# The opening of a fused attention and MLP kernel, reordered slice by slice

## The chip, the cores and the metric

The kernel runs on one core of a Trainium2 chip. A core has five engines, each with its own instruction stream: TensorE (PE, matrix products; its weight loads are listed apart as PEld), VectorE (DVE), ScalarE (ACT), GpSimd (POOL) and SyncE (SP, which here only starts transfers). They meet through semaphores. The time is that of one execution on the device, in microseconds (us); lower is better. Three executions of the kernel before took 1382.28, 1385.5 and 1387.74 us, so the median is 1385.5 us.

## The reference

One normalized input feeds a 32-head attention block and an MLP; both results are added to the input. S is 2048 tokens, D is 640, a head has 20 columns, the MLP's inner width is 1536.

```python
def _A_ref(x, wqkv, wo):                      # attention
    qkv = (x @ wqkv).reshape(B, S, 3, H, Dh).transpose(2, 0, 3, 1, 4)
    q, k, v = qkv[0], qkv[1], qkv[2]
    scores = jnp.einsum("bhqd,bhkd->bhqk", q, k) * (Dh ** -0.5)
    p = _softmax(scores, axis=-1)
    o = jnp.einsum("bhqk,bhkd->bhqd", p, v)
    return o.transpose(0, 2, 1, 3).reshape(B, S, D) @ wo

def _B_ref(x, w1, b1, w2, b2):                # MLP on a second layer norm
    y = _layernorm(x, axis=-1)
    h = _gelu(jnp.einsum("bsd,df->bsf", y, w1) + b1)
    return jnp.einsum("bsf,fd->bsd", h, w2) + b2

xn = _layernorm(x, axis=-1)
return x + _A_ref(xn, A_wqkv, A_wo) + _B_ref(xn, B_w1, B_b1, B_w2, B_b2)
```

## The kernel before

The inputs are 32-bit floats. For the projections each 32-bit factor is split into two 16-bit parts, a high part (written by ACT as a rounded copy) and a low part (written by DVE as the difference), and a product is the sum of three passes: high by high, high by low, low by high (`PASS`, line 275). A weight is first multiplied by a power of two that follows from its sum of squares.

The program has two parts. The first (lines 155 to 509) projects to Q, K and V; the second (from line 512) is attention, with the MLP and the output projection woven in. Both are written under a manual schedule: every engine runs its instructions in the order in which the text issues them, and what holds an instruction back is only a semaphore of another engine or of a transfer. A tile is taken from a pool with a fixed number of buffers, so a new tile may have to wait for the readers of an old one.

In the first part the 2048 tokens go in four chunks `c` of 512, a chunk as four row tiles `j` of 128 tokens. The steps of a chunk:

- `norm_a` (line 220): mean and variance of each row tile on DVE, a power on POOL. `norm_b` (236): one Newton step, then the four row tiles are normalized in place on DVE (line 243), then three small operations that prepare the second layer norm, the last of them a power on POOL (247). `norm_c` (249): a Newton step for the second norm and a small write by SP.
- `transp` (256) transposes normalized rows on PE into a PSUM tile, two column blocks `k` of 128 at a time; `transp_out` (266) writes high and low parts into `xnts[c]`.
- `qk(c, tt)` (277): one tile of the projection, 256 of the 1280 columns of Q and K, as 2 blocks `i` by 5 blocks `k` by 3 passes, 30 matmuls. Tiles 0 and 1 are columns of Q alone, tile 2 takes the last 128 columns of Q and the first 128 of K. `qk_out` (293): high part on ACT, low part on DVE, squares, and two writes by SP to a scratch in DRAM. `lengths` (313) sums the squares of the tiles that are pending, on PE.
- `vproj` and `vproj_out` (343, 355): the same for V, one row tile at a time.

Before a weight can be split (`split_qkv`, 379), its sum of squares is taken on ACT (`sums`, 368) and turned into a scale (`scale_of`, 371): a matmul with ones on PE (line 110) and seven small operations on DVE (from line 111).

`warm(n)` (205) gives PE n products of ones whose result isn't used; each is two matmul instructions in the profile. The opening (lines 444 to 459) is: filler, statistics of chunk 0, sum for Q, normalization, transposes, scale for Q, filler, the three feature outputs, and then Q's whole split, in five slices of 640 columns. In the main loop, chunk 0, `tt = 0` holds K's sum, `norm_c(0)` and K's scale; `tt = 1` holds K's split, `norm_a(1)` and the load of the MLP's second weight into the buffer in which K's weight stood; `tt = 2` holds V's sum, `norm_b(1)` and V's scale; from `tt = 2` on the transposes of the next chunk follow each tile. PSUM pool `psS` has three buffers of two banks, `psM` and `psO` one bank each.

`brow` (line 202) is a row constant which POOL fills (446) and which SP writes out at line 458.

Of the kernel before, what the change touches and what calls it, by code (L numbers as in the profile page):

```python
# [7 lines left out]
F32 = mybir.dt.float32  # L8
F16 = mybir.dt.float16
BF16 = mybir.dt.bfloat16  # L10
# [6 lines left out]
P = 128  # L17
# [25 lines left out]
def mha_mlp_kernel(tc, x, wqkv, wo, w1, b1, w2, b2, out):  # L43
# [4 lines left out]
    with (  # L48
# [106 lines left out]
        with tc.tile_pool(name="pa", bufs=2) as pa, tc.tile_pool(name="pa1", bufs=1) as pa1, tc.manual_schedule():  # L155
# [39 lines left out]
            for m in range(KD):  # L195
# [4 lines left out]
                                        compare_op=ALU.is_ge, fill=0.0, base=DH - 1 - m * P,  # L200
                                        channel_multiplier=-1)
            brow = pa1.tile([H, S], F16, name="brow")
            lmx = pa1.tile([P, 2, 4], F32, name="lmx")

            def warm(n):
# [30 lines left out]
            def norm_b(c):  # L236
                mv, ve, r, r2 = rs[c]
                newton(r, ve, "a")

                nc.vector.tensor_mul(ve, r, r)  # L240
                nc.vector.tensor_scalar(r, r, 1024.0, None, ALU.mult)
                for j in range(4):
                    nc.vector.tensor_scalar(xts[c][j], xts[c][j], mv[:, j, 0:1], r[:, j : j + 1],
                                            ALU.subtract, ALU.mult)
                nc.vector.tensor_mul(ve, ve, mv[:, :, 1])
                nc.vector.tensor_scalar(ve, ve, EPS, None, ALU.add)
                nc.gpsimd.tensor_tensor(r2, ve, nhalf, ALU.pow)
# [26 lines left out]

            PASS = ((0, 0), (0, 1), (1, 0))

            def qk(c, tt):
                ps = psS.tile([P, 2, 512], F32, tag="s", name="qkp")
                order = [(i, k) for i in range(2) for k in range(KD)]
                if c + tt == 0:  # L280

                    order = [(i, k) for k in range(KD) for i in range(2)]
                for i, k in order:
                    q, mm = divmod(2 * tt + i, KD)
                    for n, (a, b) in enumerate(PASS):
                        nc.tensor.matmul(ps[:, i, :], wv[:, k, q, a, mm * P : (mm + 1) * P],  # L286
                                         xnts[c][:, k, b, :], start=(k + n == 0), stop=(k == KD - 1 and n == 2))
                return ps

            norms = [None, None]  # L290
# [2 lines left out]
            def qk_out(c, tt, ps):  # L293
                hl = stp.tile([P, 2, 2, 512], F16, tag="ks", name="qkhl")

                parts = ((0, 2),) if tt != 2 else ((0, 1), (1, 2))
                sq = pa.tile([P, 2, 512], BF16, tag="sq", name="sq", bufs=2)
                for i0, i1 in parts:
                    a = qks[:, (2 * tt + i0) // KD : (2 * tt + i0) // KD + 1]
                    nc.scalar.activation(hl[:, 0, i0:i1], ps[:, i0:i1], AF.Copy, scale=a)  # L300
                    nc.vector.scalar_tensor_tensor(hl[:, 1, i0:i1], ps[:, i0:i1], a, hl[:, 0, i0:i1],  # L301
                                                   ALU.mult, ALU.subtract)
                if c == 0:
                    nc.scalar.activation(sq, hl[:, 0], AF.Square)
                else:
                    nc.vector.tensor_mul(sq, hl[:, 0], hl[:, 0])
                for s in range(2):
                    nc.sync.dma_start(
                        qkscr[s, 2 * tt * P : (2 * tt + 2) * P, c * 512 : (c + 1) * 512]
                        .rearrange("(i p) t -> p i t", p=P), hl[:, s])  # L310
                pend.extend((c, 2 * tt + i, sq[:, i]) for i in range(2))

            def lengths():
# [54 lines left out]
            def sums(tag, ws):  # L368
                accs[tag] = squares(ws, junk)
# [6 lines left out]
                    q = "qk".index(tag)  # L376
                    nc.vector.tensor_scalar(qks[:, q : q + 1], pw[tag][0], QKTOP, 2.0**-22, ALU.min, ALU.mult)

            def split_qkv(n):
                q = "qkv".index(n)  # L380
                for k in range(KD):
                    nc.scalar.activation(wv[:, k, q, 0], stage[n][:, k], AF.Copy, scale=scales[n])
                    nc.vector.scalar_tensor_tensor(wv[:, k, q, 1], stage[n][:, k], scales[n], wv[:, k, q, 0],
                                                   ALU.mult, ALU.subtract)

            gscale, f1, f2, ch, fo, big = (sc[:, i : i + 1] for i in range(6))

# [55 lines left out]

            warm(40)
            norm_a(0)
            nc.gpsimd.memset(brow, KROW)
            sums("q", [stage["q"][:, 0:3], stage["q"][:, 3:]])
            norm_b(0)
            pts = []
            transp(0, 0, pts)  # L450
            scale_of("q")
            transp(0, 2, pts)
            transp(0, 4, pts)
            warm(12)
            for t in pts:
                transp_out(*t)
            split_qkv("q")
            nc.sync.dma_start(bscr[H : H + 1, :], brow[0:1, :])
            nc.sync.dma_start(b1t, b1.rearrange("(k p) -> p k", p=P))
            for c in range(4):  # L460
                nxt = c + 1 if c < 3 else None
                for tt in range(5):
                    ps = qk(c, tt)
                    lengths()

                    if c == 0:
                        if tt == 0:
                            sums("k", [stage["k"][:, 0:3], stage["k"][:, 3:]])
                            norm_c(0)
                            scale_of("k")  # L470
                        elif tt == 1:
                            split_qkv("k")
                            norm_a(1)
                            nc.sync.dma_start(w2t, w2.rearrange("(k p) n -> p k n", p=P))
                        elif tt == 2:
# [607 lines left out]
```

## Time and profile before

| what | value |
|---|---|
| median of three executions | 1385.5 us |
| the profiled execution, its own time | 1385.2 us |
| its span (first to last instruction) | 1383.5 us |
| mean granted TensorE clock over the span | 0.997 |
| ACT busy | 1126.2 us (81%) |
| DVE busy | 1061.7 us (77%) |
| moved by DMA | 125.68 MB |
| first matmul of the projections | 21.16 us |
| first scores of attention | 232.47 us |

The engines' busy times overlap, so they don't add up to the span. Times in the timeline are microseconds from the span's start. A group's row gives its busy time, the mean time of one instruction in nanoseconds, and behind the second bar the idle time of its engine just before it with what ended most of that. In a timeline row the part in brackets is the idle time before the row and its releaser. Matmul ends are modelled.

### The profile page before, as it was taken

The page shows a single profiled execution, that of the slowest core. Times are in us where ns is not written, and L with a number is a line of the kernel's source. Part 1 is how long each engine was busy: PE and PEld are TensorE (multiplying, and loading weights), DVE is VectorE, ACT ScalarE, POOL GpSimd, SP SyncE. Part 2 cuts the span into 40 slices and gives each one's busy share as a digit, 9 for nine tenths or more (in the row PEclk, how much of TensorE's full clock was granted, in tenths as well). Part 3 has the DMA queues.
Part 4 walks back from the last instruction along what each step waited for, and adds up shares of the span by engine and source line. Part 5 has one row for each costly group of instructions (what it writes and reads, how often), then busy time and mean ns, then how long its engine had stood idle before and what let it go on. Part 6 is the DMA issues. An engine that isn't in the chain of part 4 may idle for free.

```text
span 1383.5 us, 29113 instructions
## 1 busy us (share of the span) xinstructions
PE 1350.8 (98%) x11711; PEld 600.9 (43%) x11711; DVE 1061.7 (77%) x1425; ACT 1126.2 (81%) x1282; POOL 32.9 (2%) x75
## 2 busy tenths in 40 slices
PE   9999999999999999999999999999999999999998
PEld 6555555443333343433343333343334334333375
DVE  6648743899778977889887789877988897888642
ACT  5644323999999999999999999999999999999700
POOL 2000000000000000000000000000000000000000
PEclk9999999999999999999999999999999999999999
DMA  9853413012124231213221123212124322341375
GB/s 265 243 175 109 108 52 110 16 32 64 41 55 111 67 88 34 69 52 102 71 77 33 47 75 103 76 47 58 44 64 113 98 56 70 85 153 59 98 235 179
DMA packets 92320, 125.68 MB, mean 91 GB/s; under 512 B 16905, under 2 KB 58569, under 8 KB 92178
## 3 DMA queue, kind: packets, MB, share of 16 engines
q1 hardware_dynamic: 89218, 117.14, 28.3%
q0 software_dynamic: 2304, 5.24, 2.3%
q8 instruction: 94, 1.54, 0.5%
q10 hardware_dynamic: 656, 1.36, 0.3%
q14 instruction: 48, 0.39, 0.1%
HBM read 80.84 MB, written 42.86 MB: 89 GB/s over the span
## 4 chain that ended last, share of the span: by engine, by line
PE 59%; DVE 11%; ACT 5%; DMA 3%; issue 2%; SPq 1%; DVEq 0%; ACTq 0%
PE o L615 23%; PE s L584 14%; PE py L819 9%; PE pu L787 8%; DVE low L598 5%; PE z L896 5%; ACT p L586 4%; DMA oscr<-oa 1%; DVE u L740 1%; DMA oa<-opart 1%; DVE u L741 1%; DVE w L744 1%; DVE w L745 1%; DVE hT L752 1%; DVE u L750 1%
## 5 line engine op out<-in xcount | busy, mean ns | idle before, releaser
L586 ACT ACTIVATE p<-s 128x1024 f32<-128x1024 f32 x1024 | 973.6, 1042 | 52.4 <-PE s L584 46.2
L598 DVE TENSOR_TENSOR low<-p 128x1024 f16<-128x1024 f32 x512 | 608.8, 1219 | 165.0 <-ACT p L586 164.9
L615 PE MATMUL o<-p,vfull 128*32 128x512 bf16 (+1 forms) x4096 | 433.7, 494 | 0.0
L584 PE MATMUL s<-qs,ks 61*128 61x512 f16 x2048 | 317.7, 382 | 8.7 <-ACT p L586 7.2
L584 PEld LDWEIGHTS <-ks 61*128 61x128 f16 x2048 | 63.9, 94 | 296.4 <-issue 294.2
L787 PE MATMUL pu<-xm,w1t 128*128 128x256 f16 x1440 | 179.2, 274 | 4.1 <-DVE u L740 3.6
L819 PE MATMUL py<-w2t,hT 128*128 128x320 f16 x1152 | 178.6, 301 | 1.7 <-DVE xb L757 1.7
L787 PEld LDWEIGHTS <-w1t 128*128 128x128 f16 x1440 | 130.9, 98 | 71.2 <-issue 57.6
L819 PEld LDWEIGHTS <-hT 128*128 128x128 f16 x1152 | 102.5, 98 | 89.5 <-issue 55.2
L286 PE MATMUL qkp<-xnt,wv 128*128 128x512 f16 x600 | 132.3, 380 | 0.0
L615 PEld LDWEIGHTS <-vfull 128*32 128x32 f16 x3072 | 61.5, 95 | 146.2 <-issue 115.4
L615 PE MATMUL o<-low,vfull 128*32 128x512 f16 x1024 | 107.3, 379 | 6.6 <-DVE low L598 6.4
L300 ACT ACTIVATE qkhl<-qkp,qks 128x1024 f16<-128x1024 f32 (+1 forms) x24 | 23.3, 971 | 84.1 <-PE qkp L286 66.2
L286 PEld LDWEIGHTS <-wv 128*128 128x128 f16 x600 | 58.2, 98 | 67.8
L615 PEld LDWEIGHTS o<-p,vfull 128*32 128x32 f32 x2048 | 63.1, 109 | 50.6 <-issue 0.5
L349 PE MATMUL vp<-wv,xnt 128*128 128x320 f16 x480 | 66.6, 300 | 0.0
L896 PE MATMUL z<-w1t,ot 128*128 128x320 f16 x480 | 65.8, 300 | 0.0
L896 PEld LDWEIGHTS <-ot 128*128 128x128 f16 x480 | 46.7, 98 | 19.8 <-issue 1.7
L349 PEld LDWEIGHTS <-xnt 128*128 128x128 f16 x480 | 46.5, 98 | 18.2
L301 DVE SCALAR_TENSOR_TENSOR qkhl<-qkp,qks,qkhl 128x1024 f16<-128x1024 f32 (+1 forms) x24 | 26.5, 1104 | 34.3 <-ACT qkhl L300 34.3
L857 DVE SCALAR_TENSOR_TENSOR acc<-z,sc,acc 128x320 f32<-128x320 f32 x32 | 17.6, 550 | 45.1 <-PE z L896 42.9
L636 ACT ACTIVATE ev<-o 128x512 f32<-128x512 f32 x64 | 39.4, 615 | 3.3 <-PE o L615 3.3
(168 smaller groups left out, 685.7 us busy)
## 6 DMA issues: line engine op xcount, KB each, us to landing
qkscr<-qkhl SPq DMA_DIRECT2D x40, 256.0 KB
opart<-ev SPq DMA_DIRECT2D x124, 80.0 KB
ks<-qkscr SPq DMA_DIRECT2D x120, 80.0 KB
qs<-qkscr SPq DMA_DIRECT2D x192, 40.0 KB
oa<-opart SPq DMA_DIRECT2D x32, 240.0 KB
xt<-in_A_x_dram SPq DMA_DIRECT2D x16, 320.0 KB
xscr<-xnt SPq DMA_DIRECT2D x4, 1280.0 KB
xm<-xscr SPq DMA_DIRECT2D x8, 640.0 KB
```

Source lines behind the costliest of these rows:

```text
L286: nc.tensor.matmul(ps[:, i, :], wv[:, k, q, a, mm * P : (mm + 1) * P], xnts[c][:, k, b, :], start=(k + n == 0), stop=(k == KD - 1 and n == 2))
L300: nc.scalar.activation(hl[:, 0, i0:i1], ps[:, i0:i1], AF.Copy, scale=a)
L301: nc.vector.scalar_tensor_tensor(hl[:, 1, i0:i1], ps[:, i0:i1], a, hl[:, 0, i0:i1], ALU.mult, ALU.subtract)
L349: nc.tensor.matmul(ps[:, hf, :320], xnts[c][:, k, a, j * P : (j + 1) * P], wv[:, k, 2, b, hf * 320 : (hf + 1) * 320], start=(n == 0), stop ...
L584: nc.tensor.matmul(ps[:, a, :], ks[64 * a : 64 * a + 61, kb * P : (kb + 1) * P], qs[64 * a : 64 * a + 61, cc * 512 : (cc + 1) * 512], star ...
L586: nc.scalar.activation(pt, ps, AF.Exp, scale=QS)
L598: nc.vector.tensor_sub(low, pt, upper(pt))
L615: nc.tensor.matmul(pv.o[32 * q : 32 * q + 32, :], src[:, v0 - PAD * (1 - q % 2) :][:, :32], t, start=q not in pv.begun, stop=last, skip_gr ...
L636: nc.scalar.activation(evs[g, hf][:, cc], pv.o, AF.Copy)
L787: nc.tensor.matmul(ps[:, i], w1v[:, k, (f + i) // 4, a, fo_ : fo_ + P], xnt[:, k, b, :], start=(n == 0), stop=(n == 3 * KD - 1))
L819: nc.tensor.matmul(ps[:, :320], hTs[mc][:, f, a, j * P : (j + 1) * P], w2v[:, f, b, hf * 320 : (hf + 1) * 320], start=(n == 0), stop=(n == ...
L896: nc.tensor.matmul(ps[:, :320], ot[:, k, a, j * P : (j + 1) * P], wov[:, k, b, h * 320 : (h + 1) * 320], start=(n == 0), stop=(n == 3 * KD ...
```

## The change

Some work of the opening is cut into slices and given another place:

- The fill of `brow` on POOL goes from behind `norm_a(0)` to the tile's declaration, behind the masks `heads`.
- The last three operations of `norm_b` become `norm_b2`. For chunks 1 to 3 they stay where they were; for chunk 0 they go, with `norm_c(0)`, to the start of `tt = 1`.
- Chunk 0's transposes go row tile by row tile: four blocks of a row tile together, the scale for Q ahead of the last row tile, and the fifth block of all four row tiles at the end, in a tile of `psM`. The filler behind them is 10 products instead of 12.
- Features and Q's weights come in turn: for each `k`, block `k` of the features (512 columns, high and low) and then slice `k` of Q's weights, only the 256 columns of the first tile. Columns 256 to 511 are split behind the first tile's matmuls, columns 512 to 639 in `tt = 1`.
- `tt = 0` ends after K's sum of squares. The rest of it moves into `tt = 1`, in this order: `norm_b2(0)`, `norm_c(0)`, the second tile's matmuls with K's scale issued from among them (`mid`, behind block `i = 1` of `k = 2`, so behind 18 of 30 matmuls), the first tile's `qk_out` without the squares, the last columns of Q, K's split, `lengths` (nothing is pending), the first tile's squares (`qk_sq`), `norm_a(1)`, the load of the MLP's second weight, the second tile's `qk_out`.
- The second tile's matmuls go, as the first's did, with `k` in the outer loop.

```diff
@@ -200,6 +200,7 @@
                                         compare_op=ALU.is_ge, fill=0.0, base=DH - 1 - m * P,
                                         channel_multiplier=-1)
             brow = pa1.tile([H, S], F16, name="brow")
+            nc.gpsimd.memset(brow, KROW)
             lmx = pa1.tile([P, 2, 4], F32, name="lmx")
 
             def warm(n):
@@ -242,6 +243,11 @@
                 for j in range(4):
                     nc.vector.tensor_scalar(xts[c][j], xts[c][j], mv[:, j, 0:1], r[:, j : j + 1],
                                             ALU.subtract, ALU.mult)
+                if c > 0:
+                    norm_b2(c)
+
+            def norm_b2(c):
+                mv, ve, r, r2 = rs[c]
                 nc.vector.tensor_mul(ve, ve, mv[:, :, 1])
                 nc.vector.tensor_scalar(ve, ve, EPS, None, ALU.add)
                 nc.gpsimd.tensor_tensor(r2, ve, nhalf, ALU.pow)
@@ -274,10 +280,10 @@
 
             PASS = ((0, 0), (0, 1), (1, 0))
 
-            def qk(c, tt):
+            def qk(c, tt, mid=None):
                 ps = psS.tile([P, 2, 512], F32, tag="s", name="qkp")
                 order = [(i, k) for i in range(2) for k in range(KD)]
-                if c + tt == 0:
+                if c == 0 and tt < 2:
 
                     order = [(i, k) for k in range(KD) for i in range(2)]
                 for i, k in order:
@@ -285,6 +291,8 @@
                     for n, (a, b) in enumerate(PASS):
                         nc.tensor.matmul(ps[:, i, :], wv[:, k, q, a, mm * P : (mm + 1) * P],
                                          xnts[c][:, k, b, :], start=(k + n == 0), stop=(k == KD - 1 and n == 2))
+                    if mid and (i, k) == (1, 2):
+                        mid()
                 return ps
 
             norms = [None, None]
@@ -294,20 +302,25 @@
                 hl = stp.tile([P, 2, 2, 512], F16, tag="ks", name="qkhl")
 
                 parts = ((0, 2),) if tt != 2 else ((0, 1), (1, 2))
-                sq = pa.tile([P, 2, 512], BF16, tag="sq", name="sq", bufs=2)
                 for i0, i1 in parts:
                     a = qks[:, (2 * tt + i0) // KD : (2 * tt + i0) // KD + 1]
                     nc.scalar.activation(hl[:, 0, i0:i1], ps[:, i0:i1], AF.Copy, scale=a)
                     nc.vector.scalar_tensor_tensor(hl[:, 1, i0:i1], ps[:, i0:i1], a, hl[:, 0, i0:i1],
                                                    ALU.mult, ALU.subtract)
+                if c + tt > 0:
+                    qk_sq(c, tt, hl)
+                for s in range(2):
+                    nc.sync.dma_start(
+                        qkscr[s, 2 * tt * P : (2 * tt + 2) * P, c * 512 : (c + 1) * 512]
+                        .rearrange("(i p) t -> p i t", p=P), hl[:, s])
+                return hl
+
+            def qk_sq(c, tt, hl):
+                sq = pa.tile([P, 2, 512], BF16, tag="sq", name="sq", bufs=2)
                 if c == 0:
                     nc.scalar.activation(sq, hl[:, 0], AF.Square)
                 else:
                     nc.vector.tensor_mul(sq, hl[:, 0], hl[:, 0])
-                for s in range(2):
-                    nc.sync.dma_start(
-                        qkscr[s, 2 * tt * P : (2 * tt + 2) * P, c * 512 : (c + 1) * 512]
-                        .rearrange("(i p) t -> p i t", p=P), hl[:, s])
                 pend.extend((c, 2 * tt + i, sq[:, i]) for i in range(2))
 
             def lengths():
@@ -376,12 +389,12 @@
                     q = "qk".index(tag)
                     nc.vector.tensor_scalar(qks[:, q : q + 1], pw[tag][0], QKTOP, 2.0**-22, ALU.min, ALU.mult)
 
-            def split_qkv(n):
+            def split_qkv(n, ks=range(KD), c0=0, c1=D):
                 q = "qkv".index(n)
-                for k in range(KD):
-                    nc.scalar.activation(wv[:, k, q, 0], stage[n][:, k], AF.Copy, scale=scales[n])
-                    nc.vector.scalar_tensor_tensor(wv[:, k, q, 1], stage[n][:, k], scales[n], wv[:, k, q, 0],
-                                                   ALU.mult, ALU.subtract)
+                for k in ks:
+                    nc.scalar.activation(wv[:, k, q, 0, c0:c1], stage[n][:, k, c0:c1], AF.Copy, scale=scales[n])
+                    nc.vector.scalar_tensor_tensor(wv[:, k, q, 1, c0:c1], stage[n][:, k, c0:c1], scales[n],
+                                                   wv[:, k, q, 0, c0:c1], ALU.mult, ALU.subtract)
 
             gscale, f1, f2, ch, fo, big = (sc[:, i : i + 1] for i in range(6))
 
@@ -443,33 +456,51 @@
 
             warm(40)
             norm_a(0)
-            nc.gpsimd.memset(brow, KROW)
             sums("q", [stage["q"][:, 0:3], stage["q"][:, 3:]])
             norm_b(0)
-            pts = []
-            transp(0, 0, pts)
-            scale_of("q")
-            transp(0, 2, pts)
-            transp(0, 4, pts)
-            warm(12)
-            for t in pts:
-                transp_out(*t)
-            split_qkv("q")
+            xnts[0] = pa.tile([P, KD, 2, 512], F16, tag="xnt", name="xnt0")
+            pts = [psS.tile([P, 2, 512], F32, tag="s", name="pt") for _ in range(2)]
+            pt = [pts[0][:, 0], pts[0][:, 1], pts[1][:, 0], pts[1][:, 1]]
+            for j in range(4):
+                if j == 3:
+                    scale_of("q")
+                    pt.append(psM.tile([P, 512], F32, tag="m", name="pt4"))
+                for k in range(KD - 1):
+                    nc.tensor.transpose(pt[k][:, j * P : (j + 1) * P], xts[0][j][:, k * P : (k + 1) * P], ident)
+            for j in range(4):
+                nc.tensor.transpose(pt[4][:, j * P : (j + 1) * P], xts[0][j][:, 4 * P :], ident)
+            warm(10)
+
+            for k in range(KD):
+                nc.scalar.activation(xnts[0][:, k, 0, :], pt[k], AF.Copy)
+                nc.vector.tensor_sub(xnts[0][:, k, 1, :], pt[k], xnts[0][:, k, 0, :])
+                split_qkv("q", [k], 0, 2 * P)
+            nc.sync.dma_start(xscr[:, :, :, :512], xnts[0])
+            del xts[0]
             nc.sync.dma_start(bscr[H : H + 1, :], brow[0:1, :])
             nc.sync.dma_start(b1t, b1.rearrange("(k p) -> p k", p=P))
             for c in range(4):
                 nxt = c + 1 if c < 3 else None
                 for tt in range(5):
-                    ps = qk(c, tt)
+                    if c == 0 and tt == 1:
+                        norm_b2(0)
+                        norm_c(0)
+                        ps = qk(0, 1, lambda: scale_of("k"))
+                        hl = qk_out(0, 0, first)
+                        split_qkv("q", c0=4 * P)
+                        split_qkv("k")
+                    else:
+                        ps = qk(c, tt)
                     lengths()
 
                     if c == 0:
                         if tt == 0:
+                            split_qkv("q", c0=2 * P, c1=4 * P)
                             sums("k", [stage["k"][:, 0:3], stage["k"][:, 3:]])
-                            norm_c(0)
-                            scale_of("k")
+                            first = ps
+                            continue
                         elif tt == 1:
-                            split_qkv("k")
+                            qk_sq(0, 0, hl)
                             norm_a(1)
                             nc.sync.dma_start(w2t, w2.rearrange("(k p) n -> p k n", p=P))
                         elif tt == 2:
```

## The prediction

> **What bounds the kernel now.** I read the page first: span, busy shares and the chain that ended last.
>
> ```profile
> span 1383.5 us, 29113 instructions
> PE 1350.8 (98%) x11711; PEld 600.9 (43%) x11711; DVE 1061.7 (77%) x1425; ACT 1126.2 (81%) x1282; POOL 32.9 (2%) x75
> PE 59%; DVE 11%; ACT 5%; DMA 3%; issue 2%; SPq 1%; DVEq 0%; ACTq 0%
> ```
>
> PE is the engine to watch, but a share is an average over stages, so the next view is the busy time of each engine by stretch, in the projection stage that the change opens (columns: stretch, its length, then PE, PEld, DVE, ACT, POOL, granted clock, DMA share, GB/s).
>
> ```profile
> 20.00:28.00 8.00, 8.00 (x46) 4.42 (x46) 4.56 (x10) 5.49 (x9) 0.00 (x0) 1.00 0.97 331
> ...
> 40.00:45.00 5.00, 4.41 (x29) 2.14 (x28) 4.58 (x20) 0.69 (x1) 1.17 (x2) 1.00 0.96 341
> ...
> 60.00:65.00 5.00, 5.00 (x44) 3.38 (x43) 2.17 (x3) 4.60 (x6) 0.00 (x0) 1.00 0.78 228
> ...
> 140.00:145.00 5.00, 5.00 (x31) 2.15 (x30) 4.89 (x10) 1.83 (x2) 1.18 (x1) 1.00 0.14 44
> ```
>
> PE runs without a gap except in 40 to 45 us, where DVE is busy 4.58 of 5: the one place near the opening where DVE, not PE, sets the pace. Whatever DVE loses before it, PE pays there; behind it PE is full again, so what PE loses there reaches the end.
>
> Third, the timeline of the opening (start, length, engine, line, what):
>
> ```profile
> 1.07 11.38 PE L209 MATMUL warm<-ones 128*128 128x128 f32 x80 [1.07 <-POOL ones L174]
> ...
> 12.83 2.18 DVE L243 TENSOR_SCALAR xt<-xt,mv,r 128x640 f32<-128x640 f32 x4
> ...
> 13.59 1.92 PE L262 MATMUL pt<-ident,xt 128*128 128x128 f32 x8 [1.14 <-DVE xt L243]
> ...
> 15.49 2.41 PE L262 MATMUL pt<-ident,xt 128*128 128x128 f32 x12
> ...
> 17.69 3.63 PE L209 MATMUL warm<-ones 128*128 128x128 f32 x24
> ...
> 19.88 4.06 DVE L383 SCALAR_TENSOR_TENSOR wv<-w1t,s_q,wv 128x640 f16<-128x640 f32 x5
> ...
> 21.16 6.64 PE L286 MATMUL qkp<-xnt,wv 128*128 128x512 f16 x30
> ```
>
> The first projection starts at 21.16, right where the filler (`warm`) ends: the first low slice of Q's weights is written at 19.88 + 0.88 = 20.8, and each further one comes faster (0.8 us) than PE uses it (six matmuls, 6 x 6.64/30 = 1.33 us). So filler and clock gate the start, the weights hardly.
>
> Fourth, what follows K's scale, up to the next chunk's transposes:
>
> ```profile
> 22.07 1.79 ACT L94 ACTIVATE junk<-w2t 128x1920 bf16<-128x1920 f32 x1
> ...
> 25.17 0.18 ACT L94 ACTIVATION_READ_ACCUMULATOR junk<-w2t 128x1 f32 x1
> ...
> 27.63 0.28 PE L110 MATMUL mxp<-acc,ones 128*128 128x2 f32 x2
> ...
> 27.95 0.16 DVE L111 TENSOR_REDUCE lo_k<-mxp 128x1 f32<-128x2 f32 x1 [3.34 <-PE mxp L110]
> ...
> 29.03 1.27 DVE L301 SCALAR_TENSOR_TENSOR qkhl<-qkp,qks,qkhl 128x1024 f16<-128x1024 f32 x1
> ...
> 30.79 4.07 DVE L383 SCALAR_TENSOR_TENSOR wv<-w2t,s_k,wv 128x640 f16<-128x640 f32 x5 [0.48 <-ACT wv L382]
> ...
> 34.77 0.88 DVE L230 BATCH_NORM_STATS2 st<-xt 128x6 f32<-128x320 f32 x2
> ...
> 38.98 1.28 DVE L301 SCALAR_TENSOR_TENSOR qkhl<-qkp,qks,qkhl 128x1024 f16<-128x1024 f32 x1
> ...
> 41.15 0.30 PE L321 MATMUL norms<-sq,heads 128*32 128x128 bf16 x8
> ...
> 41.37 0.38 PE L110 MATMUL mxp<-acc,ones 128*128 128x2 f32 x2
> 41.39 2.18 DVE L243 TENSOR_SCALAR xt<-xt,mv,r 128x640 f32<-128x640 f32 x4
> ...
> 42.15 1.91 PE L262 MATMUL pt<-ident,xt 128*128 128x128 f32 x8 [0.39 <-DVE xt L243]
> ...
> 43.96 1.24 PE L286 MATMUL qkp<-xnt,wv 128*128 128x512 f16 x5
> ```
>
> This is a chain without slack. DVE waits 3.34 us for K's sum on PE at 27.95, and then never stops: scale, first tile out, K's split, statistics of chunk 1, second tile out, its normalized rows at 41.39. PE waits 0.39 us for those rows. A microsecond added between 27.95 and 41.39 moves the transposes at 42.15 by a microsecond.
>
> **The change, part by part.** Prices of slices come from two sizes of one operation:
>
> ```profile
> L301 DVE SCALAR_TENSOR_TENSOR qkhl<-qkp,qks,qkhl 128x1024 f16<-128x1024 f32 x4 | 5.1, 1278 | 3.4 <-ACT qkhl L300 3.4
> ...
> L269 ACT ACTIVATE xnt<-pt 128x1024 f16<-128x1024 f32 x4 | 4.1, 1014 | 2.5 <-PE pt L262 2.5
> ...
> L382 ACT ACTIVATE wv<-w1t,s_q 128x640 f16<-128x640 f32 x5 | 3.7, 825 | 0.0
> ...
> L301 DVE SCALAR_TENSOR_TENSOR qkhl<-qkp,qks,qkhl 128x512 f16<-128x512 f32 x2 | 1.5, 750 | 0.8 <-ACT qkhl L300 0.8
> ...
> L269 ACT ACTIVATE xnt<-pt 128x512 f16<-128x512 f32 x2 | 1.2, 586 | 0.0
> ```
>
> DVE: (1278 - 750)/512 = 1.03 ns a column; a 640-column split advances 4.06/5 = 0.81 us, so 256 columns 0.41 and 128 columns 0.28. ACT: (1014 - 586)/512 = 0.84 ns; 3.7/5 = 0.74 us, so 0.42 and 0.31.
>
> Start of the first projection. With four blocks transposed per row tile, PE works in the gaps in which it waited for DVE's rows (0.52 us apart); eight transposes need no time later, but the last ones run at half clock in both kernels (below): I take 0.3 us. Two fillers fewer are four matmuls at 11.38/80 = 0.142 = 0.57. So 21.16 - 0.87 = 20.3. Bounds: 0 (the clock rises later) and 1.4 (it never falls). The data are there: the scale of Q, 1.0 us behind the sum's matmul (27.95 to 29.03 for K), comes at about 16.7; then ACT needs 0.5 + 0.42 a slice and DVE 0.56 + 0.41, so pair k is ready at 17.9 + 0.97k, far ahead of 20.3 + 1.33k.
>
> Columns 256 to 511 of Q: ACT from 21.4 to 23.5, DVE to some 24.3, while PE works on the first tile until 20.3 + 6.64 = 26.9: nothing on the path; without that cover up to 2.1 us.
>
> Step c of the norm and the second half of step b, now after those slices: two operations, the power on POOL (1 us), four operations, DVE done by about 26.6. It then waits for K's sum, so they are free. The two copies, the two write-outs on SP and K's sum of squares (22.07 to 25.4, so 3.3 us; now 23.5 to 26.8) meet the same wait.
>
> K's scale is the costly step. Its matmul moves from behind the first tile to behind 18 of the 30 matmuls of the second. Queued behind its reading on DVE, in program order: the first tile's low half, the last Q columns, K's split, chunk 1's statistics, the second tile's low half, chunk 1's rows. Summed against 27.95 to 42.15: start -0.87; 18 x 6.64/30 = +3.98; five 128-column splits of Q, put between tile and K, 5 x 0.28 = +1.40; the wait of 0.48 for ACT at 30.79 is gone, since ACT starts K's split at the scale (about 32.1) and leads DVE by 2.6. Together +4.0: scale reading at 31.1, K's split 34.8 to 38.8, statistics at 38.7, rows at 45.4, transposes at 46.1. The third tile on PE isn't starved: it needs the Q columns from 33.9 (ready from 33.7, 0.28 apart against 0.66 in use) and the last K slice at 39.8 (ready 38.8). Bounds of this sum: +3.0 if the start gains 1.4 and a split of 128 costs only its columns (0.13 x 5 = 0.66 in place of 1.40 leaves 2.7; I round up for the ACT work beside it), +5.3 if the start gains nothing and ACT's last Q slice waits for PE's second tile (0.45).
>
> PE, in its turn, arrives early: 20.3 + 90 x 0.221 + 0.7 for norms and sum = 40.9. It idles some 5.0 us where it idled 0.39. What that does to the clock shows earlier in this trace:
>
> ```profile
> 15.90:16.00 0.10, 0.10 (x4) 0.10 (x2) 0.10 (x1) 0.10 (x1) 0.10 (x1) 0.62 0.20 77
> ...
> 19.30:19.40 0.10, 0.10 (x3) 0.10 (x3) 0.10 (x2) 0.10 (x2) 0.00 (x0) 0.81 1.01 359
> ```
>
> PE stood from 12.45 to 13.59 and then only transposed at DVE's pace; at 15.93 the clock fell to one half and rose at 19.33, after 1.6 us of filler. Here the gap is four times as long, so I expect the fall, and a rise at a step of 3.4 us that has at least 1.6 us of matmuls before it: 1.6 to 5.0 us behind the fourth tile's start at 43.96 + 4.0 = 47.9. Half of that is lost: 0.8 to 2.5, middle 1.65; below it nothing, if the clock holds.
>
> The memset: the last POOL mask ends at 7.3, so 1.8 us later it is 9.1, and DVE asks for the power at 9.3:
>
> ```profile
> 7.09 0.21 POOL L199 TENSOR_SCALAR_AFFINE_SELECT heads<-heads 128x32 bf16<-128x32 bf16 x1
> ...
> 9.37 1.04 POOL L233 TENSOR_TENSOR r<-ve,nhalf 128x4 f32<-128x4 f32 x1 [2.08 <-DVE ve L232]
> 10.38 1.79 POOL L446 MEMSET brow<- 32x2048 f16 x1
> ...
> 34.88 0.38 SPq L474 DMA_DIRECT2D w2t<-in_B_w_dram  x1
> ...
> 62.92 1.26 ACT L415 ACTIVATE junk<-w2t 128x1280 bf16<-128x1280 f32 x1
> ```
>
> Nothing was waiting for it where it was, and it just fits where it goes: 0. On SP the load of the MLP's second weight waits for K's split (34.88 becomes 38.9), the first tile's two writes ahead of it move by 3; the first reader, at 62.92, is tied to PE and moves by as much, so its margin stays.
>
> Sum against the profiled execution: 1385.2 (span 1383.5 and 1.7 around it) + 4.0 + 1.65 = 1390.8. The median of the runs, 1385.5, is 0.3 above that execution, so I say 1391. About 0.5% (6.9 us) is what a measurement of this kernel can tell from no change.
>
> **The rivals.** (1) *The clock holds.* For it: between 42 and 44, where PE had gaps of 0.3 to 0.4 us, no stretch shows a lower clock. Against it: 5 us against gaps that small. Then only the chain counts: 1385.5 + 4.0 = 1389.5.
>
> (2) *Slower by more than 0.5%: the clock stays low for longer.* If transposes don't help to raise it and a whole step of matmuls is needed, the rise comes 3.4 to 6.8 us behind 47.9 and costs 1.7 to 3.4; with a start that gains little, 1385.5 + 4.4 + 3.4 = 1393.3. It passes 0.5% where chain and clock together exceed 6.9. Against it: at 19.33 the filler had run for only half a step. The Trainium skill, TensorE: Matmul & The Clock Gate, section What's actually happening, says that the clock halves after an idle window of about 3.4 us and returns after a busy one, the windows running free; its section PE-mode transpose says that transposes don't count as busy. The fall at 15.93 and the rise 3.4 us later agree with it; by it alone the loss would be 1.7 to 3.4, this rival's.
>
> (3) *Not slower: the start's gain survives.* It would need the 4.0 us on DVE to be hidden, with statistics of chunk 1 (4.2 us, 34.77 to 38.98) run in the time in which DVE waits for K's sum, 26.6 to 31.1. Then the transposes come at about 42 and 0.9 or less is kept: 1384.6. It decides from the point where DVE reads K's sum no later than 27.1. Against it: DVE's order in the trace is that of the text, and in the changed text the statistics come after K's split.
>
> **How the numbers follow.** Forecast (chain and part of a clock step, +4.9 to +6.9) 0.40; clock holds (+3 to +4.9) 0.20; slower by over 0.5% 0.30; start's gain survives 0.10, of which more than 0.5% faster 0.02, since the whole opening before the first projection has only 21 us and its data come at 17.9. Same is 0.40 + 0.20 + 0.08 = 0.68. The range 1387.5 to 1394.5 leaves out rival 3 (0.10) and the far end of rival 2 (some 0.07).
>
> **What would show it.** First projection at about 20.3; second tile at 26.9; K's first reduce on DVE at 31.1 behind an idle time of some 4.5 us; 128-column splits at 0.28; K's split from 34.8; a PE wait of 3 to 4 us on DVE's rows, behind the sum for V, ending at 46.1; half clock for 1.6 to 5 us from about there; then the same order of work later by 4 to 6.5 us, at the start of attention too. It is wrong if K's reduce comes before 29, if DVE runs statistics ahead of K's split, or if the transposes follow the third tile without a wait.

## The result, and the profile after

The changed kernel takes 1387.64 us (median of 22 executions, 1386.52 to 1389.76), the kernel before 1385.59 us (22 executions beside them): a ratio of 1.0014, 95% interval 1.0007 to 1.0020. That is 2.05 us or 0.14% slower: within 0.5%, the class that had most of the chance, in the forecast direction, and just inside the lower end of the range (1387.5). The sum of the prediction, +5.6 us, was more than twice too large.

The profiled execution took 1389.28 us. The page's lines that answer to those shown of before:

```profile
span 1387.4 us, 29129 instructions
PE 1352.5 (97%) x11707; PEld 600.4 (43%) x11707; DVE 1062.3 (77%) x1437; ACT 1128.5 (81%) x1294; POOL 32.9 (2%) x75
PE 61%; DVE 10%; ACT 4%; DMA 3%; issue 2%; SPq 1%; DVEq 0%; ACTq 0%; POOLq 0%
```

Twelve instructions more on DVE and on ACT, and busy times all but unchanged: the page can't show this change, the timeline of the opening can. Rows of the changed kernel (start, length, engine, line; three dots stand for rows left out; lines here are those of the changed kernel, so 396 is the split of weights, 308 the write-out's low half, 231 the statistics, 244 the normalized rows, 268 the next chunk's transposes):

```profile
7.25 1.79 POOL L203 MEMSET brow<- 32x2048 f16 x1
...
10.64 0.17 DVE L218 TENSOR_SCALAR at<-at 128x4 f32<-128x4 f32 x1
...
11.44 2.18 DVE L244 TENSOR_SCALAR xt<-xt,mv,r 128x640 f32<-128x640 f32 x4
...
15.37 2.40 PE L210 MATMUL warm<-ones 128*128 128x128 f32 x20
...
17.60 4.70 PE L292 MATMUL qkp<-xnt,wv 128*128 128x512 f16 x21
...
28.28 0.16 DVE L111 TENSOR_REDUCE lo_k<-mxp 128x1 f32<-128x2 f32 x1 [2.65 <-PE mxp L110]
...
29.35 1.27 DVE L308 SCALAR_TENSOR_TENSOR qkhl<-qkp,qks,qkhl 128x1024 f16<-128x1024 f32 x1
30.54 1.39 DVE L396 SCALAR_TENSOR_TENSOR wv<-w1t,s_q,wv 128x128 f16<-128x128 f32 x5
31.86 4.06 DVE L396 SCALAR_TENSOR_TENSOR wv<-w2t,s_k,wv 128x640 f16<-128x640 f32 x5
...
35.84 0.88 DVE L231 BATCH_NORM_STATS2 st<-xt 128x6 f32<-128x320 f32 x2
...
39.38 0.38 PE L110 MATMUL mxp<-acc,ones 128*128 128x2 f32 x2 [1.72 <-ACT junk L94]
...
43.21 2.17 PE L268 MATMUL pt<-ident,xt 128*128 128x128 f32 x8 [3.44 <-DVE xt L244]
45.17 8.12 PE L292 MATMUL qkp<-xnt,wv 128*128 128x512 f16 x30
...
53.21 0.29 PE L334 MATMUL norms<-sq,heads 128*32 128x128 bf16 x8
```

PE starts the first projection at 17.60, 3.56 us earlier than before. At the next chunk's transposes (43.21 against 42.15) the lead has become a delay of 1.06: PE waited 1.72 us for V's sum of squares and then 3.44 us for DVE's rows, where the kernel before waited 0.39. The fourth tile then takes 8.12 us instead of 6.63, because the clock is at one half. By its end the delay is 2.69: the row at 53.21 stands at 50.52 in the kernel before:

```profile
50.52 0.29 PE L321 MATMUL norms<-sq,heads 128*32 128x128 bf16 x8
```

Granted clock of the changed kernel (the last but two column), by half microseconds:

```profile
41.00:41.50 0.50, 0.00 (x0) 0.00 (x0) 0.47 (x3) 0.00 (x0) 0.22 (x1) 0.82 1.03 415
...
44.50:45.00 0.50, 0.50 (x4) 0.32 (x3) 0.43 (x4) 0.00 (x0) 0.01 (x1) 0.50 1.03 394
...
47.50:48.00 0.50, 0.50 (x3) 0.15 (x1) 0.50 (x1) 0.50 (x1) 0.00 (x0) 0.50 1.02 361
48.00:48.50 0.50, 0.50 (x3) 0.20 (x2) 0.12 (x1) 0.50 (x2) 0.00 (x0) 0.86 1.09 371
```

Up to attention nothing more is lost: it begins 2.68 us later (235.15 against 232.47). The spans of the two profiled executions differ by another 1.2 us behind it, where half-clock steps fall in other places (239.3 to 246.1 us after, 237.8 to 241.2 before); that these steps are the cause isn't shown. The medians, 2.05 us apart, are those of 22 executions each.

### The profile page after: what moved, and what is told of

Same layout as the page of the kernel before. It is cut to its first block, busy times and chain, and to the rows that moved or that the text cites. A ratio compares the mean times of both kernels' runs of the same rounds, so it can differ in the third digit from the quotient of the medians.

```text
span 1387.4 us, 29129 instructions
## 1 busy us (share of the span) xinstructions
PE 1352.5 (97%) x11707; PEld 600.4 (43%) x11707; DVE 1062.3 (77%) x1437; ACT 1128.5 (81%) x1294; POOL 32.9 (2%) x75
## 3 DMA queue, kind: packets, MB, share of 16 engines
q10 hardware_dynamic: 656, 1.36, 0.4%
## 4 chain that ended last, share of the span: by engine, by line
PE 61%; DVE 10%; ACT 4%; DMA 3%; issue 2%; SPq 1%; DVEq 0%; ACTq 0%; POOLq 0%
PE o L646 24%; PE s L615 15%; PE py L850 10%; PE pu L818 8%; PE z L927 5%; DVE low L629 4%; ACT p L617 3%; DMA oscr<-oa 1%; DVE u L771 1%; DVE u L772 1%; DVE w L775 1%; DVE hT L783 1%; DMA rb<-linv 1%; DVE w L776 1%; DVE u L781 1%
## 5 line engine op out<-in xcount | busy, mean ns | idle before, releaser
L646 PEld LDWEIGHTS o<-p,vfull 128*32 128x32 f32 x2048 | 62.7, 108 | 51.0 <-issue 0.5
```

The costliest lines, as they stand in the source:

```text
L646: nc.tensor.matmul(pv.o[32 * q : 32 * q + 32, :], src[:, v0 - PAD * (1 - q % 2) :][:, :32], t, start=q not in pv.begun, stop=last, skip_gr ...
```

## Where the early start came from: a row of the kernel before that the prediction passed over

The prediction priced the memset at 0, since no instruction waits for `brow`. This stretch of DVE's timeline in the kernel before says otherwise:

```profile
10.45 0.16 DVE L215 TENSOR_TENSOR at<-r 128x4 f32<-128x4 f32 x1 [1.16 <-POOL r L233]
10.65 0.16 DVE L216 TENSOR_TENSOR at<-at,ve 128x4 f32<-128x4 f32 x1
10.85 1.36 DVE L217 TENSOR_SCALAR at<-at 128x4 f32<-128x4 f32 x1
12.24 0.16 DVE L218 TENSOR_TENSOR r<-r,at 128x4 f32<-128x4 f32 x1
```

An operation on four columns takes 1.36 us, and its twin in the changed kernel (10.64 above) 0.17. POOL's fill ran from 10.38 for 1.79 us, to 12.17; DVE's operation ended at 12.21. It isn't waiting for a semaphore, so it shows as a long busy time, not as idle time with a releaser, and no view of waits lists it. The two operations ahead of it, of another kind, ran at full speed beside the same fill. The Trainium skill, SBUF — State Buffer, section Who interferes with whom, has the rule: DVE and GpSimd share a port pair, an operation of the `tensor_scalar` kind can take it, and whichever comes second is blocked to the end of the first. The rows agree, with 1.19 us. What the runs themselves show is the stop; that it is a port is the page's account.

The fill stops DVE at its new place too, where DVE comes early enough. It runs there from about 7.2 to 9.0, and the operation ahead of the power took 0.27 us in the changed kernel and 0.69 us in the run with K's scale ahead (below), here in this order:

```profile
8.81 0.27 DVE L233 TENSOR_SCALAR ve<-mv 128x4 f32<-128x4 f32 x1
...
8.36 0.69 DVE L233 TENSOR_SCALAR ve<-mv 128x4 f32<-128x4 f32 x1
```

Whenever it starts, it ends with the fill, at 9.05 to 9.08; in the kernel before, without a fill beside it, it takes 0.17 us.

### Experiment: the fill at the top of the kernel before, alone

```diff
             brow = pa1.tile([H, S], F16, name="brow")
+            nc.gpsimd.memset(brow, KROW)
...
             norm_a(0)
-            nc.gpsimd.memset(brow, KROW)
```

> The kernel before with one edit: POOL's fill of brow at the top. Port theory: in the profile before, the fill held DVE's small operation at 10.85 (1.36 us where its twins take 0.17), until the fill ended at 12.17. Then the rows come 1.2 us earlier, the first projection 1.2 or a little more (20.0), K's first reduce at 26.7, and everything behind it too: 1385.6 - 1.2 = 1384.4. Rival, my prediction's price of the memset: nothing waited for it, 1385.6 and the rows at 12.8.

Measured: 1384.37 us against 1385.87, ratio 0.9985 (0.9975 to 0.9994). DVE and then PE in this run:

```profile
11.37 0.17 DVE L218 TENSOR_SCALAR at<-at 128x4 f32<-128x4 f32 x1
...
12.17 2.18 DVE L244 TENSOR_SCALAR xt<-xt,mv,r 128x640 f32<-128x640 f32 x4
...
26.25 0.16 DVE L111 TENSOR_REDUCE lo_k<-mxp 128x1 f32<-128x2 f32 x1 [2.57 <-PE mxp L110]
```

```profile
18.85 0.59 PE L287 MATMUL qkp<-xnt,wv 128*128 128x512 f16 x2
19.88 5.35 PE L287 MATMUL qkp<-xnt,wv 128*128 128x512 f16 x24 [0.43 <-DVE wv L384]
...
40.46 1.92 PE L263 MATMUL pt<-ident,xt 128*128 128x128 f32 x8 [0.40 <-DVE xt L244]
```

The long operation is gone; K's scale and the transposes come 1.7 us earlier, and the kernel is 1.5 us faster. One moved line, the first item of the change, is the part that pays. In this profile the 1.7 us aren't the fill's alone. The rows come only 0.66 us earlier (12.17 against 12.83), since this execution's last statistics began 0.47 us later than those of the kernel before; and PE's clock didn't fall in the opening, so that the projection starts at 18.85 and not at 20.0 as expected.

### Experiment: the fill back in its old place in the changed kernel

```diff
             brow = pa1.tile([H, S], F16, name="brow")
-            nc.gpsimd.memset(brow, KROW)
...
             norm_a(0)
+            nc.gpsimd.memset(brow, KROW)
```

> The changed kernel with the fill of brow back behind the statistics of chunk 0. Port theory: the long small operation on DVE returns (1.2 to 1.4 us), the first projection comes at 18.8 or later, the next chunk's transposes at 44.4, and the time is 1387.6 + 1.2 = 1388.8, or up to 1390 where PE's clock also falls while it waits for the rows. Rival (the fill is free in either place, and the earlier start in the changed kernel comes from the slices): 1387.6.

Measured: 1389.2 us against 1385.87, ratio 1.0024 (1.0014 to 1.0034), so 1.6 us slower than the changed kernel. The long operation is back (DVE, then PE, in this run):

```profile
10.79 1.36 DVE L217 TENSOR_SCALAR at<-at 128x4 f32<-128x4 f32 x1
...
13.55 1.61 PE L469 MATMUL pt<-ident,xt 128*128 128x128 f32 x12 [1.80 <-DVE xt L243]
```

The first projection starts at 18.28 and the next chunk's transposes come at 43.90, both 0.5 us ahead of the expectation and only 0.7 us behind the changed kernel's profile. That profile's own filler ran late, until 13.18; the two runs of the next section that share its opening start their projection at 16.90 and 16.94, so against them the fill's old place costs 1.3 to 1.4 us. Both directions agree on about 1.5 us by the medians (1.3 here if each kernel is taken against the kernel before that ran beside it, and the intervals of the two ratios overlap). Without the fill's move, the rest of the change costs 3.3 us.

## Where the loss came from: K's scale

### Experiment: K's scale ahead of the second tile

```diff
-                        ps = qk(0, 1, lambda: scale_of("k"))
+                        scale_of("k")
+                        ps = qk(0, 1)
```

> The changed kernel with K's scale issued ahead of the second tile's matmuls instead of among them. Chain theory: PE waits some 1.8 us behind the first tile for K's sum of squares (24.1 to 25.9), but DVE reads it at 26.2 and not at 28.3, and all of its chain up to chunk 1's rows comes 2.1 us earlier: transposes at 41.1, and PE's wait there is 3.9 us shorter, so that the clock may hold. 1387.6 - 2.1 = 1385.5, and 1384.1 with the clock at full. Rival (PE, not DVE, sets the pace, and the wait behind the first tile is a plain loss): 1387.6 + 1.8 = 1389.4.

Measured: 1386.16 us (1383.20 to 1392.15), ratio 1.0004 (0.9992 to 1.0017), 1.5 us below the changed kernel. PE in this run:

```profile
16.90 6.64 PE L292 MATMUL qkp<-xnt,wv 128*128 128x512 f16 x30
...
25.17 0.38 PE L110 MATMUL mxp<-acc,ones 128*128 128x2 f32 x2 [1.63 <-ACT junk L94]
25.41 13.11 PE L292 MATMUL qkp<-xnt,wv 128*128 128x512 f16 x60
...
40.53 1.91 PE L268 MATMUL pt<-ident,xt 128*128 128x128 f32 x8 [1.36 <-DVE xt L244]
```

PE now stands 1.63 us for K's sum of squares, and the kernel is faster for it: DVE gets K's sum at 25.59 and is 2.7 us earlier all along its chain (0.7 of it an earlier start of this execution, 16.90 for 17.60). So DVE's chain sets the pace, as predicted, and the wait that was put on PE is no loss, since PE waits another 1.36 us for the rows behind it. By the times alone this isn't settled, as the intervals overlap (0.9992 to 1.0017, and 1.0007 to 1.0020 for the changed kernel); the rows settle it. Against the kernel before with the fill moved, the first projection starts 1.95 us earlier here (16.90 against 18.85), yet the transposes come at the same time, 40.53 against 40.46. The slices' head start is spent. In this profile the clock held through the wait; the median lies 1.7 us above this execution (1384.45). Why isn't shown: the mean granted clock is 0.995 in it and in the median of the twelve.

### Experiment: the last columns of Q ahead of the second tile

```diff
+                        split_qkv("q", c0=4 * P)
                         ps = qk(0, 1, lambda: scale_of("k"))
                         hl = qk_out(0, 0, first)
-                        split_qkv("q", c0=4 * P)
```

> The changed kernel with the split of Q's last 128 columns issued ahead of the second tile, where DVE is idle for 2.65 us, instead of between the first tile's write-out and K's split. Chain theory: 1.3 us leave the chain, K's split starts at 30.6 and the transposes at 41.9: 1387.6 - 1.3 = 1386.3, the fall of the clock as before. Rival (the first tile's write-out on ACT, now behind these slices, or the clock takes the gain back): 1387.6.

Measured: 1387.02 us, ratio 1.0005 (0.9996 to 1.0014), 0.6 us below the changed kernel (two comparisons that overlap). In this run K's first reduce stands at 27.62, with an idle time of 0.61 us ahead of it in place of 2.65, and the transposes at 41.25 (43.21 in the changed kernel). 0.66 us of that is an earlier start of this execution (16.94 against 17.60); the other 1.3 is the term of the prediction. PE then waited 2.14 us, and the fourth tile still took 8.20 us. The place of these splits costs 1.3 us in the profile; the time shows about half of it, and not beyond the intervals.

### Experiment: filler in the wait for the rows

```diff
                 nc.tensor.matmul(pt[:, :n], ones, acc, start=True, stop=True)
+                if tag == "v":
+                    for _ in range(12):
+                        nc.tensor.matmul(mxp[:, 1, :P], ones, ones, start=True, stop=True)
```

(`mxp` is the two-bank tile of which `pt` is the first half.)

> The changed kernel with 24 filler matmuls behind V's sum on PE, in the wait for chunk 1's rows (39.8 to 43.2), writing the unused half of that sum's PSUM tile. Clock theory: the rows still come at 42.5 and the transposes at 43.2, but the fourth tile runs at full clock, 6.64 us in place of 8.1: 1387.6 - 1.4 = 1386.2. Rival (the clock falls anyway, since 1.7 us before V's sum and the transposes stay idle for it, or the filler outlasts the wait): 1387.6 or up to 0.5 more.

Measured: 1385.61 us against 1385.5, ratio 1.0001 (0.9992 to 1.0010): 2.0 us below the changed kernel, with intervals that overlap a little. PE in this run:

```profile
39.14 2.92 PE L114 MATMUL mxp<-ones 128*128 128x128 f32 x24
42.72 1.92 PE L272 MATMUL pt<-ident,xt 128*128 128x128 f32 x8 [0.66 <-DVE xt L248]
44.53 6.64 PE L296 MATMUL qkp<-xnt,wv 128*128 128x512 f16 x30
```

The same wait, filled with products that nobody uses, and the fourth tile runs in 6.64 us, with the granted clock at 1.00 through the whole opening. This prices the clock's fall at 1.5 us in the tile itself. Nor does the fall belong to one profile alone: the mean granted clock of an execution has a median of 0.994 over the 22 of the changed kernel, 0.997 over the 11 here, and 0.996 over 35 of the kernel before. Two half-clock steps of 3.4 us are worth 0.0025 of the span.

## Taking the work out of the chain, and what came next

### Experiment: statistics of chunk 1 ahead of K's scale

```diff
                         norm_b2(0)
+                        norm_a(1)
                         norm_c(0)
...
                             qk_sq(0, 0, hl)
-                            norm_a(1)
```

> The changed kernel with the statistics of chunk 1 (4.2 us on DVE) issued ahead of K's scale, in front of the last Newton step, where DVE is idle for 1.1 and 2.65 us. Chain theory: K's first reduce slips by some 0.5 us to 28.8, but what follows is 4.2 shorter, so rows at 38.7, transposes at 39.4, and PE's wait 3.8 us shorter: 1387.6 - 3.8 = 1383.8, and 1382.4 if the clock then holds. Rival (the later K split starves the third tile, and PE loses there what it gains): 1387 or more.

Measured: 1385.66 us (1381.99 to 1392.91), ratio 1.0008 (0.9993 to 1.0022). PE, then ACT, in this run:

```profile
39.49 0.38 PE L110 MATMUL mxp<-acc,ones 128*128 128x2 f32 x2 [1.88 <-DVE xt L244]
39.74 1.27 PE L268 MATMUL pt<-ident,xt 128*128 128x128 f32 x8
40.90 6.63 PE L292 MATMUL qkp<-xnt,wv 128*128 128x512 f16 x30
...
58.31 0.30 PE L334 MATMUL norms<-sq,heads 128*32 128x128 bf16 x8 [3.06 <-ACT sq L321]
```

```profile
56.06 1.11 ACT L307 ACTIVATE qkhl<-qkp,qks 128x1024 f16<-128x1024 f32 x1 [6.80 <-DMA qkscr<-qkhl]
```

(The first row names DVE, but ACT's sum for V, which the same matmul needs, ended only at 39.44.) The transposes came at 39.74, near the 39.4 expected, and half of the expected gain was taken at another place. The write-out's tile has two buffers, and the fourth tile needs the second tile's buffer, which isn't free before its writes to scratch have landed. Those are issued by SP right behind the 3840 KB load of the MLP's second weight. The kernel before has the same wait in milder form (ACT stands 1.38 us there, until 53.24). With the chain shorter, PE gets there sooner and stands 3.06 us, and the clock fell from 59 to 66 us. The runs spread over 11 us, and the profiled execution, at 1390.33, is one of the long ones. My expectation had not counted this queue.

### Experiment: the same with the load one tile later

```diff
                         elif tt == 1:
                             qk_sq(0, 0, hl)
-                            nc.sync.dma_start(w2t, w2.rearrange("(k p) n -> p k n", p=P))
                         elif tt == 2:
+                            nc.sync.dma_start(w2t, w2.rearrange("(k p) n -> p k n", p=P))
```

> The changed kernel with the statistics of chunk 1 ahead of K's scale, and the load of the MLP's second weight one tile later, behind the second tile's writes to scratch. Buffer theory: in the run without the second move ACT waited 6.80 us for those writes, which lay behind the 3.84 MB load, and PE 3.06 us for ACT's squares, and half a clock step followed. Both go: 1385.7 - 3.1 - 0.5 = 1382, the runs closer together. Rival (some write waits behind the load wherever it is, now the third tile's): 1385 to 1386 again.

Measured: 1383.01 us, ratio 0.9983 (0.9974 to 0.9992). The wait of PE behind ACT's squares is gone (the sums of squares behind chunk 0's last tile of Q and K stand at 56.63 and follow it at once, against 58.31), and the runs lie within 5 us. The rival has a point all the same: ACT still stands, now 7.20 us until 59.34 for the third tile's writes, which lie behind the moved load; only PE no longer waits for it. In this profiled execution the clock fell after all behind the wait of 1.88 us for V's sum and among the transposes (0.50 from 41 to 44 us, fourth tile 8.27 us); in the run without the second move the same gap left it at full.

### Experiment: the same moves without the slices

First the kernel before with the fill at the top and the statistics ahead:

```diff
                             norm_c(0)
+                            norm_a(1)
                             scale_of("k")
                         elif tt == 1:
                             split_qkv("k")
-                            norm_a(1)
```

> The kernel before with the fill of brow at the top and the statistics of chunk 1 ahead of K's scale, no slices. Chain theory: DVE's rows come before PE has done its third tile, so the wait of 0.40 us and the gaps among the transposes go: 1384.4 - 1.2 = 1383.2, as fast as the changed kernel with the same move, since the slices' earlier start is then spent on waiting for K's sum or chunk 1's rows. Rival (the slices are worth their 2 us once DVE is relieved): this one stays 1.5 us or more above the other.

Measured: 1382.75 us, ratio 0.9980 (0.9968 to 0.9991), the fastest median of all. PE in this run:

```profile
39.33 0.38 PE L110 MATMUL mxp<-acc,ones 128*128 128x2 f32 x2
39.57 1.07 PE L263 MATMUL pt<-ident,xt 128*128 128x128 f32 x8
40.48 6.64 PE L287 MATMUL qkp<-xnt,wv 128*128 128x512 f16 x30
```

No wait is left there, and the eight transposes take 1.07 us in place of 1.91. The sliced kernel with the same move takes 1385.66, so the rival has even the sign wrong. Then with the load moved as well:

> The kernel before with the fill at the top, statistics of chunk 1 ahead of K's scale, and the load of the MLP's second weight one tile later; no slices. Its PE waited only 1.17 us behind ACT, so the load's move is worth 1 us at most: 1382.75 - 1.0 = 1381.8, and if the slices are worth nothing, the same as the sliced kernel with both moves (1382). Rival (the slices' earlier start, 1.9 us here, counts once DVE and the load are out of its way): the sliced one is 1.5 us below this.

Measured: 1382.92 us (1380.27 to 1387.80), ratio 0.9985 (0.9971 to 0.9999). The load's move is worth nothing that shows here. In its profile PE waited 2.43 us for ACT's squares, behind the first tile of V:

```profile
61.75 0.33 PE L322 MATMUL norms<-sq,heads 128*32 128x128 bf16 x8 [2.43 <-ACT sq L305]
```

ACT had stood 6.96 us ahead of them. The profile names PE as what ended that, not a transfer, so that a write behind the load was the cause, as the rival to the buffer theory would have it, is likely but not shown. So with DVE relieved the sliced kernel takes 1383.0 with the load moved, and the unsliced ones 1382.8 and 1382.9. The slices' earlier start isn't worth anything that these runs can tell.

## Why the prediction was right, and where it was too high

The class, the sign and the mechanism of the loss (the chain behind K's scale, then the clock) were right; the size wasn't. That the median lies in the range is partly luck. It is 0.14 us above the lower end, and 2.05 us lies in neither of the two bands that carried the range (3 to 4.9 with the clock held, 4.9 to 6.9 without). The prediction's own sign of being wrong, K's reduce before 29, came true (28.28), because of the start. By its own terms, in the two profiled executions:

| term | predicted | measured | from |
|---|---|---|---|
| start of the first projection | -0.87 | -3.56 | 17.60 against 21.16 |
| K's matmul behind 18 more | +3.98 | +3.89 | start to K's reduce: 10.68 against 6.79 |
| Q's last columns, less ACT's wait | +0.92 | +0.74 | reduce to statistics: 7.56 against 6.82 |
| statistics to transposes | 0 | -0.01 | 7.37 against 7.38 |
| clock behind the wait | +1.65 | +1.63 | 2.69 at the end of the fourth tile less 1.06 |
| sum | +5.6 | +2.7 | medians: +2.05 |

- **The step that failed is the start of the first projection, and in it the price of the memset.** "Nothing was waiting for it where it was, and it just fits where it goes: 0." The new place was judged rightly to 0.1 us (the fill ends at 9.04, and DVE's operation ahead of the power, held by it, at 9.08), the old place wrongly: there it held DVE for 1.19 us. The rows came 1.39 us earlier in the profile, and the medians of two experiments put the fill at 1.5 and 1.6 us.
- **The rest of the start, 2.2 us, is two fillers and the clock.** The fillers gave 0.45, not 0.57: from the filler's start to the projection PE took 2.23 us here and 2.68 in the run with only the fill moved. The clock gave some 1.7: from the first transpose to the projection that run, at full clock, took 5.92 us, and the kernel before 7.57. I assumed that the fall at 15.93 would come again in the changed kernel. It didn't, there or in any other run. Why is open. With the rows earlier, PE went from filler to transposes without a gap (filler to 13.18, transposes from 13.01), where it had stood from 12.45 to 13.59; but with the fill back it stood 1.80 us and the clock held too. How often the kernel before has this fall in its other executions isn't shown either. The bound that the text gave for a clock that never falls, 1.4, was right in kind, but too small, and it left out the fill.
- **The chain on DVE was right in each link:** 128-column splits at 0.28 (1.39 for five), the wait of 0.48 gone, the statistics behind K's split, PE's wait ending with the rows. The idle time before K's reduce was 2.65, not 4.5, because PE came there 2.8 us earlier than forecast (28.28 for 31.1) and DVE only 1.0. The experiments with K's scale and with Q's last columns moved the chain as its terms say.
- **The clock was right in place and price; when it rose is in part luck.** It fell in the wait, and filler in the same wait restored 6.64 us. It stayed low for two steps of 3.4 us (41.3 to 48.1) and rose 3.0 us behind the fourth tile's start, within the 1.6 to 5.0 of the forecast. That forecast took 1.6 us of matmuls in a step to be enough, as in the opening. In the run with the statistics ahead a step with 2.2 us of matmuls behind 1.2 us of idle time (59.3 to 62.7) left the clock at one half. What the rises share is that PE was busy through the whole step ahead of them, if transposes are counted: 15.9 to 19.3 in the kernel before, 44.7 to 48.1 in the changed one. The prediction says that the fall and the rise in the opening agree with the rule of the Trainium skill that it cites beside rival 2 (TensorE: Matmul & The Clock Gate, sections What's actually happening and PE-mode transpose). For the rise that doesn't hold: if a whole busy step is needed and transposes don't count, the 1.6 us of filler ahead of 19.33 were too little. So no run here shows that transposes don't count.
- **The third tile wasn't starved, the second tile's slices were ready, SP's order held**, as costed. What I didn't see is that the writes behind the big load are the next limit; PE doesn't wait for them in the changed kernel, but does in its improvements.
- Rival 3 (the start's gain survives) was priced with a gain of 0.9. With the true gain of 3.6 the chain still ate it, and 1.06 more.

## What to carry to other kernels

Look at the mean time of small operations, not only at waits: an instruction that takes eight times as long as its twins may be held by another engine's work beside it, as here by POOL's fill, and no list of releasers names that. An earlier start of the busiest engine pays only as far as the next join; here PE could start 2 us sooner, but the chain of a scale on DVE decided when it could go on. And a wait of some microseconds on PE can cost once more in the clock behind it (1.5 us here), which unused products in the wait avoided.

## What the runs showed of the hardware that was not expected

- A GpSimd fill of 32x2048 16-bit elements (1.79 us) stopped a DVE `tensor_scalar` on 128x4 floats until it ended (1.36 us in place of 0.17), and left two `tensor_tensor` on the same tiles alone (0.16 each). Started at 8.36 or at 8.81 beside the moved fill, another `tensor_scalar` ended with it all the same.
- Whether the clock falls after a short gap differs between executions with nearly the same gap: with 1.88 us before V's sum and then transposes it stayed at 1.00 in one run and fell to 0.50 for 3.4 us in another. The fall comes at another place in each profile (0.8 to 1.9 us behind the start of V's sum in four of them), so for a single run a gap of this size may be a matter of chance.
- The half clock ended only behind a step of 3.4 us in which PE was busy throughout, transposes counted: so in all seven profiles with a fall ahead of 70 us. Four steps with 1.3 to 2.2 us of work in them kept it at one half.
